# An attention and mixture-of-experts kernel on one core: who turns the first pair, which queue fetches the first rows, and what the order's planner counts for a load

## The chip, the cores and the metric

The kernel runs on one core of a Trainium2 chip. The core has five engines that work side by side, each through its own list of instructions in order: TensorE (matmul, "PE" in the profile; its weight loads are "PEld"), VectorE ("DVE"), ScalarE ("ACT"), GpSimd ("POOL") and SyncE ("SP", which here only issues DMAs). An instruction waits for semaphores of other engines or of DMAs, and all that stands behind it on its engine waits along. Times are device microseconds of the core; lower is better. The time of a kernel is the median of its runs.

## The reference

Two blocks follow each other. The first is attention over `q`, `k`, `v` of shape (8, 8, 576, 64), with a window of 32 keys; heads 0 to 3 see neighbouring keys, heads 4 to 7 every fourth key. The second is a mixture of experts on the 4608 rows of 512 that come out.

```python
scores = scale * q @ k.T                    # per batch and head
scores = np.where(masks, scores, -1e9)      # window 32, plain or with step 4
attn = exp(scores - max); attn /= attn.sum() + 1e-9
x = (attn @ v).transpose(0, 2, 1, 3).reshape(4608, 512)
logits = x @ w_gate                         # (4608, 8)
expert_idx = np.argmax(logits, axis=1)      # one expert for each row
...
h = np.maximum(x_sorted[lo:hi] @ w1[e], 0)  # w1: (8, 512, 1024)
y_sorted[lo:hi] = h @ w2[e]                 # w2: (8, 1024, 512)
...
return gate_w[:, None] * y                  # back in the rows' own order
```

All of it is float32. Which rows go to which expert depends on the data, so the kernel learns it as it runs.

## The kernel before, in words

**Attention.** A pair is one batch and one type of head (plain or with step 4), so there are 16 pairs of four heads; a unit is two heads of a pair, so there are 32 units. For each pair SyncE loads q and k (`load_whole`, L403; tile `raw`, three buffers; for the last two pairs `load_half`) and v (`load_v`, L430; one buffer for each type). The plain type's v is one DMA, except for batch 0, and the other type's is 13. VectorE turns q and k (`turn`, L552), since the scores need the head's 64 elements on the partitions. For pairs below `BY_PE` the turning would be done by `turn_pe` (L581): matmuls against the identity, six groups of 12, each copied out of the accumulator by ScalarE or VectorE (`put_turned`, L593). `BY_PE` was 0, so no pair went that way. Pairs turned by `turn` and below `QUADS`, which is 4, have both their units' scores made together in four accumulator banks (`quad`, L869), in two parts of 32 elements; a pair turned by TensorE has its scores unit by unit in one part of 64 (`heads_qk`, L602).

Then each unit goes through a chain: scores on TensorE (L625), mask and scale on VectorE (L641), the row's lowest value (L653), nine exponentials on ScalarE (L659), the reciprocal of the sums on VectorE (L670, L672), the product with it on GpSimd (`norm`, L676), turning on TensorE (L686), copies (L924), and the sum with v on TensorE (L714).

**Routing.** When a batch is done, `route` (L961) makes its logits and places its rows by expert into the DRAM tensor `bucket`: five indirect DMAs by GpSimd (L523), with seven tiny memsets between two of them to pass time (L770). After batches 1, 2, 4 and 7 (`TURNS`) it also makes tables on VectorE: which expert's full 128 rows go to which slot. Slots 0 and 1 are known after batch 1, slots 2 to 5 after batch 2, slots 6 and 7 after batch 4.

**Experts.** A slot is 128 rows of one expert. `fetch_x` (L1494) reads a slot's place from a table and issues five DMAs from `bucket`, four of 64 KB for the rows (tile `x`, three buffers; L1512) and one for gates and row numbers (L1521). Slots below `BY_POOL` would be fetched by GpSimd's queue; it was 0, so SyncE fetched all. `fetch_w` (L1535) loads an expert's 2 MB halves into `w1s` and `w2s` if they are new (L1541). VectorE turns the rows (L1547), TensorE does the two layers (L1555, L1571), and GpSimd scatters the result to the output (L1596). The eight first slots lie among the attention's units; ten pairs of slots, five singles and 14 short slots follow.

**What sets the order.** All instructions are written out by a planner on the host (`Plan`, L123). `add` names a step with its engines, its cost in us, its rank, what it comes after, what buffers it takes and how much data it moves. `write` (L228) takes, again and again, among the steps that could begin within 0.25 us of the soonest one, the one of lowest rank, and appends it to its engine's list. So a cost changes nothing but the order. A step that moves data holds SyncE in the plan for its cost; its transfer begins 0.65 x 2.5 us after the issue, lasts `moved` (longer if another queue moves at that time, by `SHARED`), and is seen 0.35 x 2.5 us later (L276 to L285). While TensorE would idle before the first slot, `write` puts in matmuls whose result nobody reads (tile `unread`, L756), which keep its clock up.

Ranks in the attention grow by 20 a pair; q and k come 35 ahead of their pair's, v 5 ahead. The first experts' weights (L545) have 60 to 67, a slot's rows on SyncE 900 and its number, on GpSimd 120 and its number.

Of the kernel before, what the change touches and what calls it, by code (L numbers as in the profile page):

```python
# [16 lines left out]
ENG = mybir.EngineType  # L17
# [30 lines left out]
SINGLES = FIRSTS + 2 * PAIRS  # L48
MOST_SLOTS = (N + E * 31) // 128
NSLOT = SINGLES + max(E, MOST_SLOTS - FIRSTS - 2 * PAIRS)  # L50
BY_POOL = 0
TAIL = SINGLES + 5

SOME = 14
# [12 lines left out]
LEAD_V = 5.0  # L67
# [12 lines left out]

QUADS = 4

BY_PE = 0
RUN, LONG = S * 4 // 128, S // 16


# [36 lines left out]
class Plan:  # L123
# [17 lines left out]
    COSTS = {"DVE": BIAS}  # L141

    APART = 0.21 * IDLE
    SHARED = 1.6

    BURST, AFTER = 1.0, 0.5
    ISSUE = {"SP": 0.41, "ACT": 0.2}
# [80 lines left out]
    def write(self):  # L228
# [7 lines left out]
        n = len(left)  # L236
        while open_:
# [9 lines left out]
            at, _, e, s = min((f for f in found if f[0] <= soon), key=lambda f: (f[1], f[0]))  # L247
# [28 lines left out]
            if s.moved:  # L276
                lanes = self.lanes[e == "POOL"]
                t = s.end - s.dmas * self.ISSUE.get(e, 0.0)
                for _ in range(s.dmas):
                    t = max(t + self.ISSUE.get(e, 0.0), lanes.pop(0))  # L280
                    begin = max(self.moving[e], t + 0.65 * self.LANDS)
                    shared = any(q != e and m > begin for q, m in self.moving.items())
                    self.moving[e] = begin + s.moved / s.dmas * (self.SHARED if shared else 1.0)
                    lanes.append(self.moving[e] + 0.35 * self.LANDS)
                self.free[e], s.end = t, lanes[-1]  # L285
            for h in s.takes:
# [71 lines left out]
def kernel(  # L358
# [10 lines left out]
    nc = tc.nc  # L369
# [60 lines left out]
    def load_v(b, ty):  # L430
        if ty == 0:
            a = v[b, 0:4]
            dst = v0.rearrange("p h n d -> p (h n) d")
            if b:
                nc.sync.dma_start(
                    dst,
                    bass.AP(
                        a.tensor, a.offset - WIN * DH, [[DH, KB], [QB * DH, 4 * NB], [1, DH]]
                    ),
                )  # L440
            else:
                nc.sync.dma_start(
                    dst[:, 1:],
                    bass.AP(
                        a.tensor,
                        a.offset + (QB - WIN) * DH,
                        [[DH, KB], [QB * DH, 4 * NB - 1], [1, DH]],
                    ),
                )
                nc.sync.dma_start(dst[WIN:KB, 0], v[b, 0, 0:QB])  # L450
            return
        for n in range(NB):
            j = max(0, QB * n - WIN)
            while j < QB * (n + 1):
                r, t = j // STRIP, j % STRIP
                m = min(STRIP - t, QB * (n + 1) - j)
                p0 = j - (QB * n - WIN)
                a = v[b, 4:8, DIL * t + r : DIL * t + r + 1, :]
                nc.sync.dma_start(
                    v1[p0 : p0 + m, n],  # L460
                    bass.AP(a.tensor, a.offset, [[DIL * DH, m], [S * DH, 4], [1, DH]]),
                )
                j += m
# [318 lines left out]
    def attention():  # L782
# [12 lines left out]
        for p, (b, ty) in enumerate(pairs):  # L795
            rank = 20.0 * p
            if p < WHOLE:
# [3 lines left out]
                    takes=hr[:1], rank=rank - LEAD_QK, moved=3.4, dmas=2,  # L801
                )
            else:
                hr = [hold("raw"), hold("raw")]
                for n in range(2):
                    got[p, n] = add(
                        "SP", 1.6, lambda e, p=p, n=n: load_half(p, n), takes=[hr[n]],
                        rank=rank - LEAD_QK + n, moved=4.8, dmas=4,
# [8 lines left out]
            if p == 1:  # L817
# [5 lines left out]
                    moved=1.5,  # L823
# [7 lines left out]
                )  # L831
            hv = hold(f"v{ty}")
            v_of[p] = hv, add(
                "SP", 0.41 if ty == 0 else 5.3, lambda e, b=b, ty=ty: load_v(b, ty), takes=[hv],
                rank=rank - LEAD_V, moved=5.3, dmas=1 if ty == 0 else 13,
            )
            hq, hk = hold("qT"), hold("kT")
            turned[p] = []
            for n in range(2 if p < BY_PE else 0):
                for m in range(3):  # L840
# [4 lines left out]
                        rank=rank - LEAD_T + n + m / 4, dense=0.17,  # L845
# [7 lines left out]
                            rank=rank - LEAD_T + n + m / 4 + 0.1,  # L853
                        )
                    )
            for n in range(0 if p < BY_PE else 2):
                for g in range(2 if p < WHOLE else 1):
# [8 lines left out]
                            rank=rank - LEAD_T + n + g / 2,  # L866
# [661 lines left out]
    def load_pair(a, engine=ENG.SP):  # L1528

        _, (ex, new) = nc.values_load_multi_w_load_instructions(  # L1530
            a, engines=[engine], min_val=0, max_val=E - 1
        )
        return ex, new

    def fetch_w(j, n):  # L1535
        dst, src = ((w1s, moe_w1), (w2s, moe_w2))[n]
        if n == 0:
            _, i, ints = where[j]
            whose[j] = load_pair(ints["pair"][:, i])
        rv, new = whose[j]  # L1540
        nc.sync.dma_start(  # L1541
            dst[home(j)], src[ds(rv, 1)].rearrange("o (c l) f -> l (o c) f", l=128), cond=new > 0
        )

# [286 lines left out]
    def pair_unit(u, last, rank0):  # L1831
# [38 lines left out]
        if u == 1:  # L1870
# [4 lines left out]
                takes=[w[n]], rank=900.0 + j + 0.1 + n / 10, moved=5.2)  # L1875
            for n in range(2)
        ]
        in_turn["ld"] = ld
        in_turn.setdefault("first_w", ld)

# [233 lines left out]
    def moe():  # L2114
# [27 lines left out]
        for j in range(TAIL):  # L2142
            if FIRSTS <= j < SINGLES:
                if (j - FIRSTS) % 2 == 0:
                    last = pair_unit((j - FIRSTS) // 2, last, rank)
                for n in range(j, j + 1):
# [4 lines left out]
            D = {}  # L2151
            ld = [
                add(
                    "SP", 1.5 - n, lambda e, j=j, n=n: fetch_w(j, n),
                    after=[known, *(firsts if j < 2 else ()), *(sent if j == 1 else ()),
                           *(in_turn["ld"] if j >= SINGLES else ())],
                    takes=[w],
                    rank=900.0 + j + 0.1 + n / 10,
                    moved=0.1 if j < 2 else 4.0,
                )  # L2160
                for n, w in enumerate(hold_w.setdefault(j, [hold("w1"), hold("w2")]))
            ]
            if j + 3 < TAIL:
                ask(j + 3)
            wl = hold_w[j]
# [158 lines left out]
```

## Time and profile before

| | |
|---|---|
| median of 3 runs | 746.16 us (745.09 to 747.28) |
| the profiled execution's own time | 744.83 us |
| its span, first to last instruction | 743.0 us |
| TensorE busy | 707.2 us (95%) |
| VectorE, ScalarE, GpSimd busy | 453.9, 275.7, 213.1 us |
| mean granted TensorE clock | 0.970 |
| moved by DMA | 192.44 MB in 139070 packets |

The profile is of one execution. Busy time of TensorE counts the `unread` matmuls too, which do no work. A row of the timeline has the start, the time from the first start to the last end of a merged run of equal instructions, engine, line, operation, tiles, how many, and in brackets the idle time before it and what ended that. A row of groups has the busy time, the mean in ns, and the idle time before. Float32 matmuls show as two records each.

### The profile page before, as it was taken

How to read it: one execution, taken by the hardware profiler on the slowest of the kernel's cores; microseconds unless marked ns; L12 is line 12 of the kernel's file. 1: busy time of each engine (PE TensorE's matmuls, PEld its weight loads, DVE VectorE, ACT ScalarE, POOL GpSimd, SP SyncE). 2: the span in 40 equal slices, each digit the busy share in tenths (PEclk: the TensorE clock that was granted, in tenths of full speed). 3: DMA queues.
4: the chain of work that ended last, by engine and by line, in shares of the span. 5: the costliest groups of instructions: out<-in, count | busy, mean ns of one | idle time of the engine just before them, and what ended most of it. 6: DMA issues, size and time to landing. Idle time of an engine off the chain costs nothing. (4 is left out here: it accounts for less than half of the span.)

```text
span 743.0 us, 21577 instructions
## 1 busy us (share of the span) xinstructions
PE 707.2 (95%) x8276; PEld 577.6 (78%) x8276; DVE 453.9 (61%) x1016; ACT 275.7 (37%) x897; POOL 213.1 (29%) x565
## 2 busy tenths in 40 slices
PE   5889898997998999999989999999999999999996
PEld 2657676866877787777779888998998989997674
DVE  6978776855886775164567847668477584840000
ACT  2767657463675677421112121121212212111111
POOL 1223343520525164354111223023132232411011
PEclk9889999996999999999999999999999999999998
DMA  9898966897889699869799696687687679879850
GB/s 256 284 325 268 254 185 164 268 306 232 190 250 302 185 309 232 293 219 355 269 343 317 202 351 231 198 314 252 229 287 251 198 265 390 278 238 351 293 197 30
DMA packets 139070, 192.44 MB, mean 259 GB/s; under 512 B 67884, under 2 KB 87086, under 8 KB 138448
## 3 DMA queue, kind: packets, MB, share of 16 engines
q1 hardware_dynamic: 124832, 145.36, 64.3%
q0 software_dynamic: 12976, 44.86, 16.6%
q8 instruction: 67, 1.10, 0.6%
q10 hardware_dynamic: 1152, 0.76, 0.4%
q14 instruction: 43, 0.35, 0.1%
HBM read 209.01 MB, written 20.22 MB: 309 GB/s over the span
## 5 line engine op out<-in xcount | busy, mean ns | idle before, releaser
L659 ACT ACTIVATE e<-e,lo 128x96 f32<-128x96 f32 x288 | 103.6, 364 | 26.4 <-DVE lo L653 16.3
L1555 PE MATMUL ph<-xt,w 128*128 128x128 f32 x832 | 102.1, 281 | 0.9 <-DVE cnt L1189 0.9
L1555 PEld LDWEIGHTS ph<-xt,w 128*128 128x128 f32 x832 | 98.9, 196 | 4.5 <-issue 3.1
L1596 POOL DMA_INDIRECT out_dram<-y,to x33 | 39.6, 1199 | 210.7 <-DVE to L2107 81.8
L1571 PE MATMUL py<-w,h 128*128 128x512 f32 x208 | 97.7, 604 | 0.0
L676 POOL TENSOR_TENSOR e<-e,rec 128x864 f32<-128x864 f32 x32 | 52.3, 1634 | 148.2 <-DVE rec L672 118.3
L625 PE MATMUL scores<-kT,qT 32*64 32x96 f32 (+1 forms) x2160 | 57.9, 261 | 17.0 <-DVE e L641 7.5
L625 PEld LDWEIGHTS scores<-kT,qT 32*64 32x64 f32 (+1 forms) x2160 | 50.6, 142 | 29.3 <-issue 23.9
L1571 PEld LDWEIGHTS py<-w,h 128*128 128x128 f32 x208 | 36.9, 192 | 33.4 <-issue 32.8
L641 DVE SCALAR_TENSOR_TENSOR e<-scores,cst 128x384 f32<-128x384 f32 (+1 forms) x128 | 45.7, 395 | 17.4 <-PE scores L625 13.4
L659 ACT ACTIVATION_READ_ACCUMULATOR e<-e,lo 128x1 f32 x288 | 54.8, 190 | 0.0
L924 ACT COPY eT<-weights 96x384 f32<-96x384 f32 x94 | 42.1, 480 | 31.6 <-PE weights L686 31.6
L714 PEld LDWEIGHTS xo<-eT,v 96*64 96x64 f32 x1280 | 40.8, 140 | 13.8 <-issue 4.4
L523 POOL DMA_INDIRECT bucket<-rows,idx x40 | 39.0, 975 | 43.4 <-DVE idx L1067 16.8
L714 PE MATMUL xo<-eT,v 96*64 96x64 f32 (+1 forms) x1280 | 45.4, 227 | 2.8 <-issue 2.3
L686 PE MATMUL weights<-cst,e 128*96 128x128 f32 x288 | 47.1, 291 | 0.3 <-ACT eT L924 0.2
L686 PEld LDWEIGHTS weights<-cst,e 128*96 128x96 f32 x288 | 32.8, 135 | 15.7 <-issue 6.5
L756 PE MATMUL unread<-idle 128*128 128x512 f32 (+3 forms) x84 | 37.7, 561 | 5.6 <-POOL idle L750 4.2
L770 POOL MEMSET still<- 128x1 f32 x357 | 36.5, 102 | 17.7
L1956 PEld LDWEIGHTS Z<-xt,w 128*128 128x128 f32 x320 | 37.9, 192 | 2.0 <-issue 1.3
L1956 PE MATMUL Z<-xt,w 128*128 128x128 f32 x320 | 39.3, 276 | 0.0
L1963 PE MATMUL Z<-w,h 128*128 128x256 f32 x160 | 38.5, 383 | 0.0
(243 smaller groups left out, 1217.2 us busy)
## 6 DMA issues: line engine op xcount, KB each, us to landing
w<-in_moe_w_dram SPq DMA_DIRECT2D x46, 2048.0 KB, 11.7
raw<-in_moe_w_dram POOLq DMA_DIRECT2D x42, 1024.0 KB
qT<-in_moe_w_dram POOLq DMA_DIRECT2D x28, 512.0 KB
w<-in_moe_w_dram SPq DMA_DIRECT2D x8, 1024.0 KB
raw<-in_q_dram SPq DMA_DIRECT2D x14, 576.0 KB, 8.0
raw<-in_k_dram SPq DMA_DIRECT2D x14, 576.0 KB
v<-in_v_dram SPq DMA_DIRECT2D x7, 864.0 KB, 10.9
xp<-bucket SPq DMA_DIRECT2D x80, 64.0 KB, 7.1
```

The costliest lines, as they stand in the source:

```text
L523: nc.gpsimd.indirect_dma_start(out=bucket, out_offset=bass.IndirectOffsetOnAxis(ap=idx, axis=0), in_=rows, in_offset=None, bounds_check=NR ...
L625: nc.tensor.matmul(two[r][QB * half : QB * half + QB, KB * c : KB * c + KB], lhsT=qT[:, QB * n : QB * n + QB], rhs=kt[:, QB * n : QB * n + ...
L641: nc.vector.scalar_tensor_tensor(out=e[p, c0 : c0 + w], in0=sc[r][p, a : a + w], scalar=-SCALE, in1=m[p, a : a + w], op0=OP.mult, op1=OP.add,)
L659: nc.scalar.activation(out=ev[:, c], in_=ev[:, c], func=AF.Exp, bias=lo[:, c : c + 1], scale=-1.0, accum_out=den[:, c : c + 1],)
L676: nc.gpsimd.tensor_tensor(out=ev, in0=ev, in1=rec.unsqueeze(2).broadcast_to([128, NC, KB]), op=OP.mult)
L686: nc.tensor.transpose(tp[0:KB, c], ev[:, 3 * g + c], ident)
L714: nc.tensor.matmul(xo[DH * r : DH * r + DH, g, lo - half_s * g : hi - half_s * g], lhsT=v0[:, hd, n] if ty == 0 else v1[:, n, hd], rhs=eT[ ...
L924: copier(e)(S_["eT"][:, 3 * g : 3 * g + 3], S_["w", g][0:KB, 0:3])
L1555: nc.tensor.matmul(ph[:, f % 4], lhsT=w1s[home(j)][:, c, 128 * f : 128 * f + 128], rhs=xt[:, c], start=c == 0, stop=c == 3,)
L1571: nc.tensor.matmul(py, lhsT=h[:, f], rhs=w2s[home(j)][:, f], start=f == 0, stop=f == 7)
L1596: i = nc.gpsimd.indirect_dma_start(out=out, out_offset=bass.IndirectOffsetOnAxis(ap=to, axis=0), in_=y, in_offset=None, bounds_check=out.s ...
L1956: nc.tensor.matmul(to[:, f], lhsT=right[:, c, 128 * f : 128 * f + 128], rhs=left[:, c], start=not more and f == c == 0, stop=c == 1, skip_ ...
```

## The change

Four things change. `BY_PE` is 1, so pair 0 is turned by TensorE, and its scores are made unit by unit. `BY_POOL` is 6, so the rows of slots 0 to 5 are fetched by GpSimd's queue. In the plan, v costs SyncE 8.0 us (plain type) or 10.0 us instead of 0.41 or 5.3, and its transfer 1.5 us instead of 5.3; two transfers at a time cost 0.6 of the part that they share, instead of 1.6 of the whole; a slot's weights cost a little more. And in the plan the slots' weight loads come strictly one after the other, up to the first pair of slots. `W_POOL` is 0, so no weight load changes its queue.

```diff
-BY_POOL = 0
+BY_POOL = 6
+W_POOL = 0
...
-BY_PE = 0
+BY_PE = 1
...
-    SHARED = 1.6
+    SHARED = 0.6
...
                     begin = max(self.moving[e], t + 0.65 * self.LANDS)
-                    shared = any(q != e and m > begin for q, m in self.moving.items())
-                    self.moving[e] = begin + s.moved / s.dmas * (self.SHARED if shared else 1.0)
+                    alone = s.moved / s.dmas
+                    shared = max(m - begin for q, m in self.moving.items() if q != e)
+                    self.moving[e] = begin + alone + self.SHARED * max(0.0, min(alone, shared))
...
             v_of[p] = hv, add(
-                "SP", 0.41 if ty == 0 else 5.3, lambda e, b=b, ty=ty: load_v(b, ty), takes=[hv],
-                rank=rank - LEAD_V, moved=5.3, dmas=1 if ty == 0 else 13,
+                "SP", 8.0 if ty == 0 else 10.0, lambda e, b=b, ty=ty: load_v(b, ty), takes=[hv],
+                rank=rank - LEAD_V, moved=1.5, dmas=1 if ty == 0 else 13,
             )
...
     def fetch_w(j, n):
+        queue, engine = (nc.gpsimd, ENG.Pool) if j < W_POOL else (nc.sync, ENG.SP)
         if n == 0:
-            whose[j] = load_pair(ints["pair"][:, i])
+            whose[j] = load_pair(ints["pair"][:, i], engine)
-        nc.sync.dma_start(
+        queue.dma_start(
...
+        if u == 0:
+            for mine, slots in zip(ld, in_turn["slot_w"]):
+                mine.after.append(slots)
...
-                    "SP", 1.5 - n, lambda e, j=j, n=n: fetch_w(j, n),
+                    "POOL" if j < W_POOL else "SP", 1.8 - n, lambda e, j=j, n=n: fetch_w(j, n),
...
-                    moved=0.1 if j < 2 else 4.0,
+                    moved=0.1 if j < 2 else 5.2, plain=True,
                 )
...
+            ld[1].after.append(ld[0])
+            if j and j < SINGLES:
+                for a, b in zip(ld, in_turn["slot_w"]):
+                    a.after.append(b)
+            in_turn["slot_w"] = ld
```

## The prediction

> **What bounds the kernel now.** I read the page first, its rows by slices of the span, and then went down to the slices in which TensorE falls short.
>
> ```profile
> span 743.0 us, 21577 instructions
> PE   5889898997998999999989999999999999999996
> PEclk9889999996999999999999999999999999999998
> sum 134.00, PE 37.73 PEld 15.29; mean PE 5.39 PEld 2.18
> ```
>
> The first three lines are the page's: the span, the busy tenths of TensorE in slices of 18.6 us, and the clock that it was granted. From 200 us on TensorE is full nearly everywhere, so the end is set by how much TensorE work is left and how soon it is begun. Two places fall short. One is the start: the fourth line is the sum row of the stretches up to 134 us for the tile `unread` alone, the matmuls that only pass time, and 37.73 us of TensorE's time there are such filling. The other is the tenth slice (about 167 to 186 us), where the clock drops to 6 tenths. The stretches around it:
>
> ```profile
> 162.00:170.00 8.00, 5.50 (x137) 4.08 (x135) 0.05 (x1) 5.47 (x22) 0.14 (x1) 1.00 0.75 243
> 170.00:180.00 10.00, 7.14 (x88) 6.68 (x88) 7.71 (x12) 3.33 (x18) 1.63 (x1) 0.62 0.89 294
> 180.00:190.00 10.00, 10.00 (x91) 9.75 (x91) 6.22 (x23) 2.73 (x5) 1.63 (x1) 0.69 0.66 157
> 190.00:200.00 10.00, 10.00 (x249) 9.22 (x250) 7.12 (x17) 7.06 (x32) 5.15 (x18) 1.00 0.77 205
> ```
>
> The columns are the stretch, its length, then busy time of PE, PEld, DVE, ACT and POOL, the granted clock, the DMA share and GB/s. In the first VectorE works 0.05 us of 8. In the next two the clock is 0.62 and 0.69, and is whole again from 190. The timeline, by engine, says why:
>
> ```profile
> 157.62 0.39 SPq L1541 DMA_DIRECT2D w<-in_moe_w_dram  x1
> 159.38 2.25 SPq L1512 DMA_DIRECT2D x<-bucket  x4
> 163.01 6.86 SPq L1512 DMA_DIRECT2D x<-bucket  x4
> 169.95 0.71 DVE L1547 STREAM_TRANSPOSE xt<-x 128x512 f32<-128x512 f32 x1 [8.18 <-DMA x<-bucket]
> 163.94 1.88 PE L625 MATMUL scores<-kT,qT 32*64 32x96 f32 x72
> 172.67 0.55 PE L625 MATMUL scores<-kT,qT 32*64 32x96 f32 x2 [5.17 <-DVE e L641]
> 173.41 3.47 PE L625 MATMUL scores<-kT,qT 32*64 32x96 f32 x70 [0.19 <-DVE e L641]
> DMA to landing us min/median/max: 9.1/9.1/9.1
> DMA to landing us min/median/max: 1.8/1.8/1.8
> ```
>
> SyncE issues a 2 MB weight load at 157.62, and the rows of slot 2 behind it at 159.38. They land 9.1 us after issue (the first landing line is that of the line L1512 in the window 159 to 162; the second is of the group issued at 187.23, which took 1.8). VectorE has slot 2's transpose next in its fixed order and sits 8.18 us behind it. Behind that stand the attention's masks, and behind those TensorE, which idles 5.17 us, and then takes 4.02 us (0.55 and 3.47) for 72 score records that took 1.88 at 163.94.
>
> The price of this stall: TensorE idles 8.00-5.50 plus 10.00-7.14, that is 5.4 us; at the low clock it loses 7.14 x 0.38 plus 10.00 x 0.31, that is 5.8 us. **Together 11.2 us.** Nothing like it stands elsewhere after 134 us.
>
> **Part 1: the rows of slots 0 to 5 move to GpSimd's queue.** Slots 2 to 5 are exactly those behind the stall. In a queue of their own they no longer stand behind SyncE's weight loads, so I take the stall as gone: -11.2. Between bounds: all of it, or nothing, if rows and weights share the engines so that the rows land as late as now. SyncE also stops being held, 2.25 and 6.86 us for these two slots; what follows on it (q and k of a later pair at 170.51) goes out sooner, but no engine was waiting for that, so nothing is counted.
>
> The first slots start sooner too:
>
> ```profile
> 107.44 0.15 DVE L1333 CAST basei<-base 1x2 int32<-1x2 f32 x1
> 114.00 11.20 SPq L459 DMA_DIRECT2D v<-in_v_dram  x13
> 114.20 0.92 POOL L523 DMA_INDIRECT bucket<-rows,idx  x1 [0.71 <-ACT eT L924]
> 127.31 1.92 SPq L1512 DMA_DIRECT2D x<-bucket  x4
> 134.61 1.80 PE L1555 MATMUL ph<-xt,w 128*128 128x128 f32 x8 [0.89 <-DVE cnt L1189]
> 120.00:134.00 14.00, 1.21 (x3) 0.30 (x2) 0.95 0.59 161
> 130.00:140.00 10.00, 8.78 (x86) 7.78 (x83) 9.15 (x43) 3.98 (x8) 5.46 (x18) 0.83 0.64 180
> ```
>
> Slot 0's place is known at 107.6 and its last row leaves at 115.1, but SyncE is in the 13 loads of v until 125.2 and fetches at 127.31. GpSimd can fetch some ten us sooner. TensorE gains by that only what it wastes between about 120 and 134: 1.21 us of filling (sixth line) and 1.22 us idle (last line), so between 0 and 2.4; I take -1.5, as the transpose still has to pass on VectorE.
>
> What it costs: six times five DMAs on GpSimd, which also carries the attention's norms (L676) in order.
>
> ```profile
> L734 POOL DMA_DIRECT2D bucket<-blank x2 | 1.3, 652 | 0.3 <-POOL blank L492 0.3
> L523 POOL DMA_INDIRECT bucket<-rows,idx x40 | 39.0, 975 | 43.4 <-DVE idx L1067 16.8
> L676 POOL TENSOR_TENSOR e<-e,rec 128x864 f32<-128x864 f32 x32 | 52.3, 1634 | 148.2 <-DVE rec L672 118.3
> 159.34 1.63 POOL L676 TENSOR_TENSOR e<-e,rec 128x864 f32<-128x864 f32 x1 [2.80 <-DVE to L2221]
> 175.70 1.63 POOL L676 TENSOR_TENSOR e<-e,rec 128x864 f32<-128x864 f32 x1 [13.56 <-DVE rec L672]
> ```
>
> A direct DMA takes GpSimd 652 ns, one with indices 975 ns; the fetch is direct but from a computed address, so 0.65 to 0.98 each: 3.3 to 4.9 us a slot, 20 to 29 us in all. The cover is GpSimd's idle time, 148.2 us ahead of the norms, mostly waiting for VectorE's reciprocal. But the fetch is one step and cannot be cut, and gaps run from 2.80 us (at 159.34) to 13.56 (at 175.70). A fetch also waits until the rows' writes have landed, and a norm or scatter behind it waits along. I count one fetch in a gap that is too short, 4.1-2.80: +1.3. Without cover it is 4.1 a fetch, the rival below.
>
> In a sentence apart: the Trainium skill, page "DMA: Bandwidth & Descriptors", section "Issuing engines are not separate DMA queues", says that DMAs of all issuing engines end on the same 16 DMA engines and interleave, so that issuing from several saves only the issuing time. By that rule the rows land as late from GpSimd, and the stall stays; it names the rival "late anyway" below. The trace only half bears it out, since in the stalled stretch the DMA share is 0.75 and not full.
>
> **Part 2: TensorE turns the first pair.**
>
> ```profile
> 5.77 2.34 DVE L568 STREAM_TRANSPOSE qT<-raw 128x576 f32<-128x576 f32 x2 [4.33 <-DMA raw<-in_q_dram]
> 8.15 2.34 DVE L568 STREAM_TRANSPOSE kT<-raw 128x576 f32<-128x576 f32 x2
> 11.10 2.65 DVE L579 STREAM_TRANSPOSE qT<-raw 128x320 f32<-128x320 f32 x4 [0.61 <-DMA raw<-in_q_dram]
> 13.60 1.42 DVE L641 SCALAR_TENSOR_TENSOR e<-scores,cst 128x384 f32<-128x384 f32 x4
> 36.76 1.39 PE L714 MATMUL xo<-eT,v 96*64 96x64 f32 x40
> L924 ACT COPY eT<-weights 96x384 f32<-96x384 f32 x94 | 42.1, 480 | 31.6 <-PE weights L686 31.6
> cst<-c_pack ACTq DMA_DIRECT2D x2, 240.0 KB, 7.6
> ```
>
> Removed: 4.68 us of VectorE. Added: six groups of 12 matmuls, 144 records; the nearest row (40 records of like tiles in 1.39 us) gives 5.0 us at one group of records after another, and TensorE only fills there. Added too: six copies of 128x384 at about 0.48 us, on ScalarE, idle then. Pair 0's scores need half the matmuls. But VectorE's next own work, pair 1's q, waits for its data until 11.10 anyway, so most of the 4.68 us falls into waiting. Bounds: k cannot be turned before 8.15, so with half the groups behind that (2.5 us), a copy (0.5) and pair 0's shorter scores (36 records, half of the 72 that took 1.88: 0.9) the first mask starts at 12.1 at the soonest against 13.60: a gain of 1.5. The identity, loaded by ScalarE's queue behind a mask, may come as late as 7.6 us after an issue near 1.8: at 9.4, then 5.0 us of turning, a copy and the scores: 15.8, a loss of 2.2. I take 0, near the middle, since no row says when the identity lands.
>
> **Part 3: the plan's counts.** Nothing here runs on the chip; it changes the order that is written out.
>
> ```profile
> 38.18 0.33 SPq L435 DMA_DIRECT2D v<-in_v_dram  x1
> 40.84 8.00 SPq L409 DMA_DIRECT2D raw<-in_q_dram  x1
> 51.89 11.10 SPq L459 DMA_DIRECT2D v<-in_v_dram  x13
> v<-in_v_dram SPq DMA_DIRECT2D x7, 864.0 KB, 10.9
> ```
>
> After v of the first kind the next issue is stuck for 8.00 us, where the plan counted 0.41; the 13 loads of the second kind take 11.10, where it counted 5.3. It now counts 8.0 and 10.0, so 98 us more over 16 loads. By lines 277 to 285 the plan believed that the first kind lands 0.41+1.63+5.3+0.88, that is 8.2 us after issue, and now believes 8.0+1.63+1.5+0.88, that is 12.0; the last row measures 10.9. So its beliefs come nearer, and fewer instructions should be put ahead of data that is not there. The change of the shared factor, the chained weight loads and their moved times work on the same order. The bounds are wide, since a new order shifts every step: the 37.73 us of filling is what there is to win, and a few us of new waits what there is to lose. I take 0 for the sum, as no row prices an order that does not exist yet.
>
> **The sum.** 744.83 (the profiled execution; its span is 743.0) -11.2 -1.5 +1.3 +0 +0 = 733.4. The median of the runs shown, 746.16, lies 1.33 above the profiled execution, so 734.8.
>
> **The rivals.**
> *A better order as well.* If the true SyncE time lets the plan take a quarter of the 37.73 us of filling, 9.4 us, the time is 725, and 717 with half of it. For it speaks that VectorE and ScalarE both idle at times before 134; against it that the start is bound by VectorE and by arriving data, which the change does not make less.
> *Late anyway.* The rows land on GpSimd's queue as late as on SyncE's, or VectorE's order puts another late thing in their place. The 8.18 us stays, only the 1.5 remains: 744.7 to 746.2, no change. The 0.75 DMA share speaks against it.
> *GpSimd becomes the wait (slower).* The fetches stand ahead of ready norms; each exposed one delays the attention's chain by 4.1 us, and TensorE has little else until the first slots are in. It decides from the fourth exposed fetch, 16.4 us against the 12.7 won (749.9); at five, 20.5 us, the time is 746.2-12.7+20.5 = 754, and six give 758. Gaps of 2.80 speak for it, the 13.56 and the 148.2 us of idling against it. A reshuffled order that loses at the start what it won later would look alike in time.
>
> **How the numbers follow.** About 0.3% (2.2 us) is what a measurement can tell from no change. My forecast, 730 to 740, gets 0.50; the better order 0.22; late anyway 0.10; slower 0.18. So faster 0.72, the same 0.10, slower 0.18. The likeliest is 734.8. The range runs from 717, half of the filling won, to 751, just past four exposed fetches; beyond lie some 15 in 100, mostly five and six of them. The range of the faster cases alone is 717 to 740.
>
> **What would show it.** Right: no VectorE wait of over 3 us for x between 120 and 210; a clock of 0.9 or more in all stretches from 134 to 300; GpSimd's fetches at 3.3 to 4.9 us a slot; slot 0's first matmul before 130. Part 1 is wrong if the x of slots 2 to 5 still lands 9 us after issue, or if waits of ScalarE or TensorE for GpSimd's norm appear. Part 2 is wrong if the first mask moves by more than 2.2 us. The whole is wrong if TensorE's filling and idling before the first slot grow by 10 us: then the plan's order has taken what the queue gave.

## The result, and the profile after

The changed kernel takes 756.91 us (median of four runs, 752.37 to 759.14), the kernel before 746.72 us beside it (745.09 to 750.25, four runs). The ratio is 1.0144, with a 95% interval of 1.0105 to 1.0183: slower, where I forecast 734.8 us and a range up to 751. Here and below a median counts all runs of a kernel, while ratios and intervals leave out the executions that fell into a slower state of the chip, so a ratio need not be the quotient of two medians. The profiled execution took 759.14 us, with a span of 757.5 us, so 14.5 us more span than before; the medians lie only 10.2 us apart, so the two traces show a little more than the loss.

The page of the changed kernel, the same three rows as before:

```profile
span 757.5 us, 21716 instructions
PE   7878997999999898999399999999999999999995
PEclk9889998999999999999789999999999999999998
```

The low clock of the tenth slice is gone, and TensorE is full there. Instead the twentieth slice (360 to 379 us) has three tenths of work, at a clock of 7 tenths. The stretches, first of the kernel before, then of the changed one (the columns are as before; the first number behind the length is TensorE's busy time, and the third from the end is the clock):

```profile
0.00:134.00 134.00, 115.00 (x2026) 82.34 (x2026) 101.20 (x245) 82.42 (x333) 42.35 (x89) 0.92 0.87 245
134.00:200.00 66.00, 60.03 (x905) 51.85 (x907) 42.43 (x110) 32.90 (x127) 20.37 (x56) 0.87 0.87 256
200.00:340.00 140.00, 137.71 (x1802) 106.47 (x1799) 90.93 (x290) 83.14 (x291) 61.18 (x178) 0.99 0.89 259
340.00:420.00 80.00, 77.60 (x581) 64.55 (x581) 48.95 (x91) 15.58 (x29) 13.69 (x37) 1.00 0.91 310
```

```profile
0.00:134.00 134.00, 110.73 (x1942) 80.99 (x1946) 91.14 (x218) 75.00 (x299) 44.86 (x97) 0.92 0.87 255
134.00:200.00 66.00, 65.30 (x1087) 53.58 (x1081) 48.13 (x137) 45.83 (x175) 37.99 (x80) 1.00 0.87 282
200.00:340.00 140.00, 134.94 (x1777) 106.29 (x1773) 84.48 (x254) 81.67 (x283) 53.31 (x142) 0.98 0.83 233
340.00:420.00 80.00, 67.95 (x452) 57.27 (x451) 44.94 (x106) 13.16 (x24) 17.97 (x58) 0.91 0.83 287
```

From such rows I work out what TensorE loses in a stretch: the length less the busy time (idle), plus the length times what the clock lacks to 1 (cold). Before it is 29.7, 14.6, 3.7 and 2.4 us, after it is 34.0, 0.7, 7.9 and 19.2. The second stretch gained 13.9 us; the other three lost 4.3, 4.2 and 16.8. TensorE's turning adds 5.2 us of work in the first stretch. Together +16.6 up to 420 us, and behind 420 us TensorE idles 2.2 us more (8.3 instead of 6.1), against 14.5 measured for the whole span. The sum is rough: the clock is printed to two decimals, a step of which is 1.3 us in the first stretch, and idle time at a low clock counts twice. The `unread` matmuls up to 134 us hardly changed (37.44 us instead of 37.73).

The stall that I forecast to go is gone. In the timeline of the changed kernel GpSimd fetches slot 2 in 3.1 us, and VectorE's transpose of its rows, which waited 8.18 us before, has no wait in brackets (the last row):

```profile
165.39 2.42 POOL L1514 DMA_DIRECT2D x<-bucket  x4 [4.21 <-DMA bucket<-rows,idx]
167.89 0.57 POOL L1523 DMA_DIRECT2D gt<-bucket  x1
172.70 0.70 DVE L1550 STREAM_TRANSPOSE xt<-x 128x512 f32<-128x512 f32 x1
```

But these rows do not come sooner here: they are fetched at 165.39, where SyncE fetched them at 159.38, and are turned at 172.70 instead of 169.95. VectorE now comes to them later, behind other work; what the queue does by itself is asked below.

The largest loss is where the eight first slots end and the first pair of slots begins (the join, from here on). The timeline there, before:

```profile
350.63 5.28 SPq L1512 DMA_DIRECT2D xp<-bucket  x4
356.16 0.47 SPq L1820 DMA_DIRECT2D w<-in_moe_w_dram  x1
362.77 0.71 DVE L1883 STREAM_TRANSPOSE xt<-xp 128x512 f32<-128x512 f32 x1 [4.64 <-DMA xp<-bucket]
368.29 1.23 DVE L1849 TENSOR_TENSOR v<-w 128x1024 f32<-128x1024 f32 x1 [0.95 <-DMA own<-bucket]
```

and after:

```profile
356.68 0.49 SPq L1823 DMA_DIRECT2D w<-in_moe_w_dram  x1
358.04 5.74 SPq L1514 DMA_DIRECT2D xp<-bucket  x4
376.44 1.23 DVE L1852 TENSOR_TENSOR v<-w 128x1024 f32<-128x1024 f32 x1 [16.68 <-DMA own<-bucket]
377.58 0.71 DVE L1889 STREAM_TRANSPOSE xt<-xp 128x512 f32<-128x512 f32 x1
378.90 3.76 PE L1962 MATMUL X<-v 128*128 128x128 f32 x16 [12.05 <-DVE v L1852]
```

Three orders differ. On SyncE the pair's w2 (2 MB) is issued behind the rows of the pair's second slot (xp) before, and ahead of them after. On VectorE the turning of those rows stands ahead of w2's sum before, and behind it after. And GpSimd issues the first short expert's weights (4 MB) in two parts with slot 7's scatter between them before, and all at once at 355 to 360 after; w2 is summed 12.1 us after its issue before, and 19.8 after. TensorE needs the turned rows and idles 12.05 us. At the start the first mask comes at 18.71 us instead of 13.60. And once a fetch of GpSimd's holds a norm that TensorE waits for:

```profile
121.38 2.43 POOL L1514 DMA_DIRECT2D x<-bucket  x4 [4.68 <-DMA bucket<-rows,idx]
124.48 1.65 POOL L678 TENSOR_TENSOR e<-e,rec 128x864 f32<-128x864 f32 x1
126.18 0.86 PE L688 MATMUL weights<-cst,e 128*96 128x128 f32 x6 [2.79 <-POOL e L678]
```

The last row is TensorE's wait for that norm, 2.79 us.

### The profile page after: what moved, and what is told of

Same layout as the page of the kernel before. It is cut to its first block, busy times and chain, and to the rows that moved or that the text cites. A ratio compares the mean times of both kernels' runs of the same rounds, so it can differ in the third digit from the quotient of the medians.

```text
span 757.5 us, 21716 instructions
## 1 busy us (share of the span) xinstructions
PE 708.1 (93%) x8350; PEld 580.6 (77%) x8350; DVE 449.2 (59%) x1012; ACT 279.9 (37%) x903; POOL 232.1 (31%) x588
## 3 DMA queue, kind: packets, MB, share of 16 engines
q0 software_dynamic: 13936, 46.44, 16.8%
## 5 line engine op out<-in xcount | busy, mean ns | idle before, releaser
L661 ACT ACTIVATE e<-e,lo 128x96 f32<-128x96 f32 x288 | 103.9, 371 | 13.1 <-DMA v<-in_v_dram 8.0
L1574 PE MATMUL py<-w,h 128*128 128x512 f32 x208 | 95.4, 595 | 0.0
L627 PE MATMUL scores<-kT,qT 32*64 32x96 f32 (+1 forms) x2088 | 56.8, 252 | 10.2 <-issue 8.4
L627 PEld LDWEIGHTS scores<-kT,qT 32*64 32x64 f32 (+1 forms) x2088 | 48.9, 136 | 19.3 <-issue 13.3
L643 DVE SCALAR_TENSOR_TENSOR e<-scores,cst 128x384 f32<-128x384 f32 (+1 forms) x128 | 45.7, 395 | 22.3 <-PE scores L627 10.2
L661 ACT ACTIVATION_READ_ACCUMULATOR e<-e,lo 128x1 f32 x288 | 56.7, 197 | 0.0
L1656 POOL DMA_DIRECT2D raw<-in_moe_w_dram x42 | 14.9, 354 | 94.3 <-DMA raw<-in_moe_w_dram 50.9
L772 POOL MEMSET still<- 128x1 f32 x350 | 36.0, 103 | 17.3
```

Source lines behind the costliest of these rows:

```text
L627: nc.tensor.matmul(two[r][QB * half : QB * half + QB, KB * c : KB * c + KB], lhsT=qT[:, QB * n : QB * n + QB], rhs=kt[:, QB * n : QB * n + ...
L643: nc.vector.scalar_tensor_tensor(out=e[p, c0 : c0 + w], in0=sc[r][p, a : a + w], scalar=-SCALE, in1=m[p, a : a + w], op0=OP.mult, op1=OP.add,)
L661: nc.scalar.activation(out=ev[:, c], in_=ev[:, c], func=AF.Exp, bias=lo[:, c : c + 1], scale=-1.0, accum_out=den[:, c : c + 1],)
L1574: nc.tensor.matmul(py, lhsT=h[:, f], rhs=w2s[home(j)][:, f], start=f == 0, stop=f == 7)
```

## The experiments

I write P for TensorE's turning, Q for the rows in GpSimd's queue, C for the plan's counts (the time behind v, V, and the rest). Ratios are to the kernel before, run on the same chip. "Lost" is idle plus cold as above, of one profiled execution each. "Join" is the start of the pair's first product.

| run | what | ratio (95%) | lost 0-134 | 134-200 | 200-340 | 340-420 | join |
|---|---|---|---|---|---|---|---|
| | before | 1 | 29.7 | 14.6 | 3.7 | 2.4 | 364.2 |
| | after: P Q C | 1.0144 (1.0105-1.0183) | 34.0 | 0.7 | 7.9 | 19.2 | 364.9 |
| e1 | P Q C, VectorE's order at the join | 1.0103 (1.0010-1.0196) | 35.0 | 0.8 | 5.9 | 18.6 | 364.3 |
| e2 | P Q C, GpSimd's order | 1.0135 (1.0042-1.0229) | 30.9 | 0.7 | 6.4 | 11.8 | 360.2 |
| e3 | P Q C, both | 1.0161 (1.0074-1.0248) | 27.5 | 0.9 | 10.9 | 12.1 | 361.4 |
| e4 | P Q C without V | 1.0040 (0.9996-1.0085) | | | | | |
| f1 | P Q C, SyncE's order | 1.0114 (1.0063-1.0165) | 32.1 | 0.8 | 3.9 | 13.3 | 359.7 |
| f2 | Q C, SyncE's order | 0.9979 (0.9940-1.0017) | 21.8 | 2.0 | 3.1 | 14.4 | 349.6 |
| f3 | P C, SyncE's order | 1.0012 (0.9980-1.0044) | 31.6 | 1.0 | 4.4 | 11.8 | 358.3 |
| g1 | P Q C, all three orders | 1.0095 (1.0057-1.0132) | 29.6 | 0.8 | 6.8 | 9.7 | 357.9 |
| g2 | Q C, all three orders | 0.9952 (0.9921-0.9982) | 20.3 | 1.1 | 2.7 | 9.5 | 346.3 |
| g3 | P | 0.9975 (0.9939-1.0011) | 18.0 | 13.1 | 2.0 | 4.5 | 360.6 |
| g4 | Q, all three orders | 1.0005 (0.9970-1.0040) | 23.3 | 1.5 | 4.3 | 13.8 | 351.2 |
| h1 | P Q, all three orders | 0.9955 (0.9918-0.9992) | 20.6 | 0.6 | 5.9 | 12.5 | 352.4 |
| h2 | C | 0.9978 (0.9941-1.0014) | 25.2 | 4.0 | 17.3 | 5.6 | 363.7 |
| h3 | f2, short weights later | 0.9982 (0.9943-1.0021) | 32.6 | 3.7 | 0.9 | 14.2 | 354.2 |
| i1 | h1, short rows turned later | 0.9998 (0.9964-1.0031) | 17.4 | 0.1 | 7.2 | 13.5 | 351.9 |
| i2 | g2, short rows turned later | 0.9944 (0.9895-0.9993) | 30.1 | 3.5 | 0.9 | 7.7 | 351.5 |
| i3 | P Q V, all three orders | 1.0246 (1.0187-1.0305) | 32.1 | 5.2 | 4.4 | 25.4 | 369.5 |

No losses are given for e4, whose profiled execution took 758.71 us against a median of 750.93. One execution's loss up to 134 us is a rough number: g2 and i2 differ in an edit behind 340 us only, and have 20.3 and 30.1.

**First set: the orders at the join.** My theory was that the new order lost the time at the join. e1 puts the sums of w2 behind the pair's mixed x:

```diff
-                        after=[ld[n], *sent, *sums[n][-1:], *(() if n else in_turn.get("sh", ()))], takes=[h] if i == 0 else (),
+                        after=[ld[n], *sent, *sums[n][-1:], *(() if n else in_turn.get("sh", ())),
+                               *(sx[-1:] if n and u == 0 else ())], takes=[h] if i == 0 else (),
```

> The changed kernel, with one more condition in the plan: the first pair of slots sums its w2 only behind the mixed x of that pair (VectorE's order at the join as in the kernel before); TensorE, GpSimd and SyncE keep their order up to there. Theory (the rewritten order put w2's sum ahead of the second turning of the pair's rows, and w2 lands 20 us after its issue): the 12 us of TensorE idle and about 2 to 4 us of cold clock at 360 to 390 shrink to 2 to 4 us, w2 still lands 19 to 20 us after its issue, time 743 to 748 us. Rival A (GpSimd's crowd of weights is the cause, the order of VectorE only shows it): under 4 us gained, because the first product on w2 waits instead; 753 or more. Rival B (the loss is all in the start): no change, 755 to 759.

e2 puts the second layer of the first short expert, and all later short weights, behind slot 7's scatter:

```diff
+                if i == 0:
+                    wt[1].after.append(in_turn["last_first"])
+                else:
+                    wt[0].after.append(first[i - 1][3][1])
+                    wt[1].after.append(wt[0])
...
+            if j == FIRSTS - 1:
+                in_turn["last_first"] = sent_out
```

> The changed kernel, with the first short expert's second layer of weights (and the later ones) put behind slot 7's scatter on GpSimd's queue, as in the kernel before; VectorE's order is left as in the changed kernel, with w2's sum ahead of the second turning. Theory (both causes act together): w2 lands about 12 us after its issue in place of 19.8, so the stall before the pair's products shrinks by 7 to 8 us but 4 to 5 us stay; time 747 to 751. Rival A (the crowd of weights is all of it): the stall is under 2.5 us, 742 to 745. Rival B (start only): no change, 755 to 759.

e3 has both edits, and e4 undoes V alone:

> Both edits of the two kernels above on the changed kernel. Theory: the join is as before the change, the gain of the queue (12.8 us of idle and cold clock at 134 to 200) is seen less the 8 to 11 us lost at 0 to 134: 742 to 746 us, no more than 2 us from the kernel with the first edit alone. Rival A: as the split alone. Rival B: no change.

```diff
-                "SP", 8.0 if ty == 0 else 10.0, lambda e, b=b, ty=ty: load_v(b, ty), takes=[hv],
-                rank=rank - LEAD_V, moved=1.5, dmas=1 if ty == 0 else 13,
+                "SP", 0.41 if ty == 0 else 5.3, lambda e, b=b, ty=ty: load_v(b, ty), takes=[hv],
+                rank=rank - LEAD_V, moved=5.3, dmas=1 if ty == 0 else 13,
```

> The changed kernel with only the counts of SyncE's time behind v put back to the old numbers (0.41 and 5.3 us, moved 5.3). Its order has w2's sum behind the second turning and the short weights split by slot 7's scatter, as before. Theory (the counts cost nothing by themselves, the order that comes out decides): no 12 us stall at the join, 740 to 747 us. Rival C (the rows in GpSimd's queue or the turning by TensorE cost the time whatever the order): 754 to 759.

Medians: 757.42, 757.60, 759.02 and 750.93 us, with 747.74 before. My theory fell: with VectorE's order mended, and with both orders mended, nothing is gained. e2 and e3 do shorten TensorE's wait at X to 6.30 us, and in e2 w2 is summed 14.3 us after its issue instead of 19.8, but no time comes of it. The timeline of e1 says why:

```profile
355.86 0.75 SPq L1823 DMA_DIRECT2D w<-in_moe_w_dram  x1
357.46 7.69 SPq L1514 DMA_DIRECT2D xp<-bucket  x4
376.30 0.71 DVE L1889 STREAM_TRANSPOSE xt<-xp 128x512 f32<-128x512 f32 x1 [16.22 <-DMA xp<-bucket]
```

VectorE now comes to the second slot's rows first, and they themselves are late: issued behind w2 in SyncE's queue, they are turned at 376.30. It is the fault that Q removes for slots 0 to 5, made anew for the pair by SyncE's order. e4, whose order has the rows ahead of w2 by itself, already stood closer to the kernel before.

**Second set: SyncE's order, and one part undone.** The edit issues the pair's w2 in the step of the second slot's rows, right behind them; VectorE's order then comes out as before by the plan itself. It also puts all short weights behind slot 7's scatter.

```diff
-                add("SP", 3.5, lambda e, t=t: fetch_pair(u, t, D),
+                add("SP", 3.5, lambda e, t=t: (fetch_pair(u, t, D), fetch_pair_w(u, 1, D) if t and not u else 0),
...
-                    takes=[hx[t]], rank=900.0 + j + t, moved=1.4, dmas=5)
+                    takes=[hx[t]], rank=900.0 + j + t * (1 if u else 0.15), moved=1.4, dmas=5)
...
```

> The changed kernel with one thing fixed on SyncE's queue: for the first pair of slots, the second slot's rows are issued directly ahead of the pair's 2 MB w2, as in the kernel before (the changed kernel issues w2 first). VectorE's order at the join then comes out as before too, by the plan itself. New theory (the second slot's rows stood behind the 2 MB load in the same queue, so both the first edit and the second could not help): the 12 us stall at 360 to 390 falls to under 3 us and the time to 743 to 748 us, no more than 1% from the kernel before. Old theory (VectorE's order, GpSimd's crowd of weights): 754 or more, as with both edits. Rival B (loss in the start): 755 to 759.

> As the run above, but VectorE turns pair 0's q and k as in the kernel before (the queue change and the plan's counts stay). New theory with a slow start of TensorE's turning: the first mask is again at about 13.6 us in place of 18.7, and 3 to 8 us come off the run above: 737 to 743, faster than the kernel before. If the start's 5 us are hidden later (what is late there is waited for again by the router's or the rows' chain): within 2 us of the run above.

> As the first of these runs, but the six slots' rows are back in SyncE's queue (TensorE's turning and the plan's counts stay). If the queue change is worth the 12.8 us of idle and cold clock that the traces show at 134 to 200: 8 to 13 us slower than the first of these runs, 752 to 760, with a wait of VectorE for a slot's rows of 5 us or more at 120 to 210. If the gain there is given back at the join in any case: within 3 us of it.

> The kernel before with the same fixing of SyncE's queue, which there leaves the order of SyncE and VectorE at the join as it was and only puts the first short expert's weights behind slot 7's scatter. A control: within 0.5% of the kernel before, 743 to 750, by every theory; a gain or loss over that is the short weights' order and is taken off the other three.

f2 has `BY_PE = 0`, f3 has `BY_POOL = 0`. Medians: 752.98, 743.04, 746.55 and 760.50 us, with 745.13 before. f1 and f3 lie outside what I had expected of them. f4 is no control: there the pair's w2 overwrites slot 6's before the last of slot 6's eight second-layer products, which so reads the pair's weights and waits 14.6 us for them. It computes something else, and its time is not compared. In f1 the 12 us wait is gone and another has come. The timeline of f1:

```profile
388.32 1.22 DVE L1852 TENSOR_TENSOR v<-w 128x1024 f32<-128x1024 f32 x1 [9.48 <-DMA w<-in_moe_w_dram]
391.25 3.78 PE L1969 MATMUL A<-w,kT 128*128 128x256 f32 x8 [8.53 <-DVE y L2092]
```

Now VectorE waits for the second pair's weights, and TensorE for what stands behind that. f1 against f2 says that P costs 1.3% beside Q and C, f1 against f3 that Q costs 1.0% beside P and C. The third set asks whether each does so alone.

**Third set: all three orders held, and parts alone.** To the edit above comes that the merged step takes w2's buffer, that short weights need only the pair's w1, and e2's edit. g1 is P Q C, g2 Q C, g4 Q alone; g3 is the kernel before with `BY_PE = 1` and nothing else (its join is as before by itself).

> The changed kernel with all three queues at the join in the order of the kernel before: SyncE issues the second slot's rows ahead of the pair's w2, VectorE turns them ahead of w2's sums, GpSimd issues the first short expert's first layer ahead of slot 7's scatter and the second layer behind it. If the loss is the join alone: the stretch from slot 7's end to the last matmul is 373 to 376 us as before (384 in the changed kernel), time 742 to 747, the kernel before or a little under it. If the start by TensorE costs as much by itself as the last four runs say (10 us between the first and the second): 748 to 753, the same as with the rows alone.

> The same, but VectorE turns pair 0's q and k as before. By the theory that the queue change gains its 11 to 14 us up to slot 7's end and only the join gives them back: slot 7 ends near 350 and the last matmul comes 373 to 378 us later, time 731 to 738, faster than the kernel before by over 1%. If the join is bounded by the transfers whatever their order (12 MB of weights in 60 us): 740 to 745, no gain over the rows alone.

> The kernel before with only pair 0's q and k turned by TensorE (rows in SyncE's queue, old counts; its order at the join is that of the kernel before). If the turning costs 10 us by itself: 752 to 758. If it costs only the 5 us by which the first mask is later: 748 to 752. If the 5 us are hidden by what is late anyway (my prediction's part 2): within 2 us of the kernel before.

> The kernel before with only the six slots' rows in GpSimd's queue (VectorE's turning, old counts), and the join's three queues held in the order of the kernel before. My prediction's part 1 by itself: no wait of VectorE for rows over 3 us at 120 to 210, slot 7's end 9 to 13 us earlier than 364, time 733 to 740. If the counts, not the queue, removed the wait at 162 to 190 (the run without the queue had none): the wait stays or is not gained, 743 to 750.

Medians: 754.99, 743.68, 745.19 and 747.14 us, with 747.28 before. P alone costs nothing, Q alone neither gains nor costs; the three together still lose 1%. So neither P nor Q has a price of its own. g1 lies above both of its forecasts; g4 has the time of its second one but not for its reason, since the wait is gone. The rows of stretches of g3 (first two) and of g4 (last two):

```profile
0.00:134.00 134.00, 120.01 (x2124) 86.67 (x2125) 99.33 (x256) 80.54 (x316) 39.38 (x79) 0.97 0.82 243
134.00:200.00 66.00, 59.46 (x910) 49.02 (x909) 45.08 (x104) 37.81 (x150) 24.09 (x54) 0.90 0.89 272
```

```profile
134.00:200.00 66.00, 64.50 (x994) 51.35 (x991) 43.66 (x101) 36.72 (x140) 33.59 (x69) 1.00 0.98 300
340.00:420.00 80.00, 69.41 (x526) 59.87 (x525) 48.66 (x79) 13.73 (x26) 13.07 (x28) 0.96 0.77 258
```

In g3 the wait at 162 to 190 is still there (13.1 us lost). In g4 it is gone (1.5), the join comes 13.0 us earlier, and 340 to 420 loses 13.8 instead of 2.4. The gain is there and is given back, in another place. The timeline of g4 there:

```profile
347.04 0.39 SPq L1827 DMA_DIRECT2D w<-in_moe_w_dram  x1
348.27 23.28 SPq L1620 DMA_DIRECT2D own<-bucket  x12
369.35 0.31 DVE L1659 STREAM_TRANSPOSE own<-own 128x128 f32<-128x128 f32 x1 [12.83 <-DMA own<-bucket]
370.30 3.78 PE L1963 MATMUL A<-xt,w 128*128 128x128 f32 x16 [7.37 <-DVE h L1856]
```

The first short expert's rows (own) stand behind w2 in SyncE's queue, VectorE waits 12.83 us for them, and TensorE 7.37 behind VectorE.

One more thing stands in the traces there, for the kernel before (first three rows) and for g4:

```profile
341.23 0.98 POOL L523 DMA_INDIRECT bucket<-blank,padi  x1 [0.65 <-issue]
343.48 0.37 SPq L1820 DMA_DIRECT2D w<-in_moe_w_dram  x1
346.58 2.60 SPq L1512 DMA_DIRECT2D xp<-bucket  x4
330.56 0.37 SPq L1827 DMA_DIRECT2D w<-in_moe_w_dram  x1
338.16 0.98 POOL L524 DMA_INDIRECT bucket<-blank,padi  x1 [0.65 <-issue]
341.57 1.93 SPq L1513 DMA_DIRECT2D xp<-bucket  x4
SPq L1513 <- DMA bucket<-blank,padi: 9.6, 2, 9.3
```

The pair's first weights go out 12.9 us sooner in g4, but the padding that the last batch's routing writes into `bucket` only 3.1 us. The last row is of SyncE's waits in g4, with total, number and longest: it waits 9.3 us for these writes, so the pair's rows go out only 5.0 us sooner, and w2 and the short rows stand behind them. The DMA share at 340 to 350 is 0.56, where it was 1.00. In h1, f2 and i2 SyncE waits 9.6, 8.8 and 8.3 us at the same place. No run moves the routing, so what this wait costs is not shown.

A rival is open too. With f4 out, no run has the held orders by themselves. g3 and h2 (in the next set), whose joins needed no holding, lose 4.5 and 5.6 us at 340 to 420; f3 and g1, held and with joins not much earlier, lose 11.8 and 9.7. So the holding itself may cost some of what is lost there.

**Fourth set: turning against counts, and the stretch behind the join.** h1 is P Q with all three orders held; h2 is C alone; h3 is f2 with the short weights behind the second pair's weights (and w2's buffer taken as in the third set):

```diff
-        in_turn.setdefault("first_w", ld)
+        if u == 1:
+            in_turn["first_w"] = ld
```

> The kernel before with TensorE's turning and the six slots' rows in GpSimd's queue, but the old counts; the join's queues held in the order of the kernel before. If the turning clashes with the plan's new counts: idle and cold clock up to 134 us 17 to 23 us as with turning alone, time 738 to 746. If it clashes with the queue (GpSimd's fetches hold the norms behind them): 28 us or more up to 134 us, time 750 to 756 as with all three.

> The kernel before with only the plan's counts changed (VectorE's turning, rows in SyncE's queue); its join has the second rows ahead of w2 by itself. If the counts alone remove the wait at 162 to 190, as the run without the queue suggests: idle and cold clock at 134 to 200 under 4 us (14.6 in the kernel before), time 740 to 747. If the queue is needed for that: 10 us or more there, 745 to 750.

> As the run with the rows ahead of w2 and VectorE's turning (f2), but the first short expert's 4 MB of weights are issued only behind the second pair's weights. If the 4 MB in GpSimd's queue beside SyncE's w2 and the second pair's weights make the stretch behind slot 7 longer: idle and cold clock of the 60 us behind slot 7 fall from 15 to under 6 us, time 733 to 739. If the order of the transfers doesn't matter there: 740 to 745.

Medians: 747.84, 746.34 and 746.92 us, where the kernel before took 748.65. h1 gains 0.45%: the turning and the queue do not clash by themselves. Nor do the turning and the counts (f3, 1.0012) or the queue and the counts (g2, 0.9952): only the three together lose. Up to 134 us h1 lost 20.6 us, as forecast for it. h2 loses 4.0 us at 134 to 200: the counts alone remove most of the wait there, without the queue; but another has come, at 272 us, behind a key of a later pair:

```profile
269.93 2.23 DVE L565 STREAM_TRANSPOSE kT<-raw 128x1152 f32<-128x1152 f32 x1 [9.54 <-DMA raw<-in_k_dram]
272.21 1.88 PE L627 MATMUL scores<-kT,qT 64*64 64x96 f32 x36 [7.54 <-DVE den L672]
```

h3 loses 14.2 us at 340 to 420, f2 14.4. The short weights' place is not what stretches that time.

**Fifth set.** i1 and i2 turn the first short expert's rows behind the pair's mixed hidden sums (on h1 and g2); i3 is h1 with V alone.

```diff
-                xt = add("DVE", 0.3, lambda e, i=i: across_short(i), after=[ld, *ended], uses=[hx],
+                xt = add("DVE", 0.3, lambda e, i=i: across_short(i), after=[ld, *ended, *(() if i else in_turn["sh0"])], uses=[hx],
...
+        in_turn.setdefault("sh0", sh)
```

> As h1 (turning and queue, old counts, join held), but VectorE turns the first short expert's rows only behind the first pair's mixed hidden sums. If the wait for these rows is what stretches the time behind slot 7: the 4.2 us of TensorE idle before the pair's A products go, and the time falls by 4 to 8 us against h1, to about 0.985 to 0.99 of the kernel before. If the transfers are the bound there whatever VectorE's order: within 2 us of h1.

> The same edit on g2 (queue and counts, VectorE's start), where VectorE waited 4.2 us for these rows and TensorE hardly behind it. First reading: 0 to 3 us less than g2. Second: the same as g2.

> As h1, with the new count of SyncE's time behind v (8 and 10 us) and nothing else of the counts. If this count is what clashes with the turning and the queue: 1.005 to 1.012 of the kernel before, with 28 us or more of idle and cold clock up to 134 us. If it is the rest of the counts (the shared-transfer rule and the weights' chain): 0.993 to 1.000.

Medians: 746.61, 744.41 and 766.38 us, with 747.19 before. i1 gains nothing on h1. In its timeline VectorE, free of the short rows, waits for w2 itself, and TensorE's 4.2 us become 2.4 there, beside 6.1 at the pair's second product (4.9 in h1):

```profile
359.92 3.75 PE L1963 MATMUL X<-v 128*128 128x128 f32 x16 [6.08 <-DVE v L1856]
369.73 1.23 DVE L1856 TENSOR_TENSOR v<-w 128x1024 f32<-128x1024 f32 x1 [8.83 <-DMA w<-in_moe_w_dram]
371.62 2.05 PE L1963 MATMUL A<-xt,w 128*128 128x128 f32 x16 [2.35 <-DVE h L1856]
```

i3 is the slowest of all, twice as far off as I had expected at most: with P and Q, the true time behind v alone turns 0.9955 into 1.0246. Its losing stretches:

```profile
0.00:134.00 134.00, 115.26 (x1999) 84.25 (x2000) 94.86 (x226) 76.47 (x310) 44.80 (x97) 0.90 0.90 266
340.00:420.00 80.00, 63.42 (x390) 52.10 (x391) 51.99 (x162) 12.34 (x23) 23.23 (x76) 0.89 0.66 227
```

g2, i2 and h1 are the fastest: 0.9952, 0.9944 and 0.9955. Each keeps the queue and the join's order of the kernel before, and has either the turning or the counts, not both. Half a per cent is little, though: their intervals only just leave out 1, and i1, which differs from h1 in one order at the join, shows 0.9998.

## Why the prediction was wrong

**The stall at 162 to 190, priced at 11.2 us, did go.** It measured 13.9 between 134 and 200, VectorE had no wait of over 3 us for x at 162 to 200 (one of 3.86 at 128), and the clock was 1.00 there. All runs with Q in the table have it gone (0.1 to 5.2 us lost). But Q is not needed for it: C alone takes the loss to 4.0, P and C to 1.0.

The Trainium skill, page "DMA: Bandwidth & Descriptors", section "Issuing engines are not separate DMA queues", says that a second issuing engine saves only the issuing time. The traces bear that out more than my reason for part 1. What Q alone saved is time ahead of the issue: in g4 GpSimd fetches slot 2 at 148.32; in the kernel before SyncE, held for 12.70 us by a load of q from 142.93 on, came to it at 159.38. Next to a weight load, rows in a queue of their own were hardly quicker, as one case in h1 shows:

```profile
156.75 0.40 SPq L1543 DMA_DIRECT2D w<-in_moe_w_dram  x1
158.34 1.78 POOL L1513 DMA_DIRECT2D x<-bucket  x3 [0.70 <-issue]
168.13 0.71 DVE L1549 STREAM_TRANSPOSE xt<-x 128x512 f32<-128x512 f32 x1 [2.86 <-DMA x<-bucket]
```

VectorE waits for these rows and turns them 9.8 us after their first issue, where it was 10.6 before (159.38 to 169.95). For the bulk the rule holds too: with 4 MB in GpSimd's queue beside SyncE's w2, 19.8 us passed from issue to sum instead of 12.1.

**The step that failed first is "nothing like it stands elsewhere".** The question was what is late next, and I answered it for the slots only. Q alone brings the join 13.0 us forward and ends where it did (1.0005): 340 to 420 gives 11.4 us back (with the orders at the join held), in waits for the pair's rows, the short expert's rows and the weights, whichever the order puts first. In every run whose join came before 356, that stretch lost 7.7 to 14.4 us, against 2.4 before. The edits moved that wait from one transfer to the next (12.05 us at X, 8.53 at A, 7.37 at the other A, 6.08 at X). That it is bounded by arriving transfers is what these waits say. In g4 the first of them start late because the last batch's routing comes only 3.1 us sooner; how much of the 11.4 us is that, how much the bytes behind it and how much the held orders, no run tells apart.

**The step that failed most is part 3, "I take 0 for the sum, as no row prices an order that does not exist yet".** With P and Q the counts turn 0.9955 (h1) into 1.0095 (g1), or 1.0144 with the join as the plan writes it; V alone gives 1.0246. Alone (0.9978), with Q (0.9952) or with P (f3, 1.0012) they cost nothing. Up to 134 us the eight traces with P and V lose 27.5 to 35.0 us, the three with P and the old counts 17.4 to 20.6; f3 loses 31.6 there too, and makes it up later. So part of their cost lies in the start, as far as single traces tell; in i3 the join loses as much again (25.4 us instead of 12.5 in h1). Why truer beliefs give a worse order is not settled: the runs show which count does it, not by which decision of the plan. My reason, that nearer beliefs mean fewer instructions ahead of data, was no reason for a greedy order.

**Part 2, taken at 0 within -1.5 and +2.2.** The turning was priced right: 5.2 us, from 8.91, where I allowed for 9.4. The bound was wrong, since the first mask came at 18.71 and not by 15.8: the groups of k came one by one at 11.89, 13.49 and 15.10, and the plan gave the last two copies to VectorE, behind pair 1's q (14.46 and 16.18). I had put all six on ScalarE. But P alone is 0.9975, with its first mask at 17.56: the lateness of the first mask is no loss by itself, so the 0 was right for the wrong reason, and the first mask was a bad thing to watch.

**The rest.** A fetch takes 3.0 us instead of 3.3 to 4.9. The rival "GpSimd becomes the wait" was there, with one norm held (2.8 us against my 1.3), too small to be the cause. Nor did my sign for a start taken over by the plan's order show: up to 134 us the filling fell by 0.3 us and the idle time grew by 4.3, not by 10. "Slots start sooner", -1.5: slot 0's first matmul did come before 130, at 129.23, and the next only at 140.72, so nothing came of it.

## What to carry to other kernels

A stall that is removed is worth what the next late thing leaves of it: ask of every later stretch whether it can take its data that much earlier, and try the part alone, with the rest of the order held. When an edit makes a greedy planner rewrite the order, compare the order on each queue at every seam before pricing anything, above all where a small load slips behind a big one. A truer count in such a planner is a change like any other, to be tried alone and with its neighbours.

## What the runs showed of the hardware that was not expected

Four 64 KB fetches and a small one with computed addresses took GpSimd 3.0 us (552 ns the usual 64 KB fetch), less than the 652 ns of its other direct DMAs in the kernel before. Twelve small loads of 16 KB behind a 2 MB load held SyncE's queue for 10 to 23 us (23.28 in g4). And the same instructions up to the join lost 20.3 us up to 134 us in one execution and 30.1 in another (g2 and i2), most of the difference in the clock (4.0 and 10.7 us), so that a start is not to be judged by one trace.
